# Wider first pieces of the MLP weights, and a fourth MLP unit ahead of the folds

One Trainium2 chip, one core of it. The metric is the device time of one execution in microseconds (us); an execution takes some 1.7 us more than the span of its instructions in the trace, and the tables say which is meant.

## The reference

A layer norm feeds two branches over the same 2048 tokens of width 640, and the sum of both with the residual is the output.

```
xn = layernorm(x)                                # x: 1 x 2048 x 640, bf16
# branch A: linear attention, 32 heads of 20
q, k, v = split(xn @ wqkv)
pq, pk  = q @ w_phi, k @ w_phi                   # per head, 20 x 20
phi(p)  = concat(softmax(p), softmax(-p))
o       = phi(pq) @ (phi(pk)^T v) / (phi(pq) @ sum(phi(pk)))
A       = o @ wo
# branch B: gated MLP, 1536 columns
B       = (silu(xn @ w1) * (xn @ w3)) @ w2
out     = x + A + B
```

The kernel folds w_phi into wq and wk (a "fold" multiplies a transposed 128-column chunk of wk with the block-diagonal w_phi), so that k and pk need one projection. A V tile is the ten matmuls that give v for 128 tokens, a K tile the ten that give pk for 128 tokens. A DMA transfer "lands" when all of its data has arrived.

## The kernel before

The program declares operations with a priority and lets its own list scheduler, with a model of durations and a random seed, put them into one order per engine at build time. On the chip that order is fixed. One MLP unit is ten matmuls: 128 columns of w1 and 128 of w3 against 512 tokens of xn transposed.

```
def mlp(b, fc, level):
    ...
    for j, w in enumerate((w1_s, w3_s)):
        for i in range(DC):                      # DC = 5 chunks of 128 rows
            mm(j, lambda k, j=j: bank(k + j), w[:, i, fc * 128:(fc + 1) * 128],
               xnT[:, i, b * 512:(b + 1) * 512], i == 0, i == DC - 1)
        ...                                      # tanh on ScalarE, products on VectorE
```

The head of the load order on the one SyncEngine queue, which is where the change sits:

```
    load_wv(4, 5, lv - 3)
    on_act(2.65, load_x, 3, 4)
    n = len(P.all)
    load_w13(0, 384, lv - 4)                     # first piece of w1, then of w3
    for d in P.all[n:]:
        d.raw.add(chunk)                         # not before the first piece of wv
    first = [P.all[n]]
    for e in range(DC):
        o = load_wT(1, e, lv - 9 - e, first)     # wk, transposed by the DMA; waits for w1's piece
        if e == 1:
            load(phi_s[:], phi_t, lv - 10.5, "SP", first)
    load_x(4, 8, lv - 19, "SP", [o])             # not before the last wk
    n = len(P.all)
    load_w13(384, 768, lv - 20)
    load_x(8, 12, lv - 21)
    ...
        if t in TURNED:                          # TURNED = (0,): tile 0 of xn
            turn(xnT[:, :, t * 128:(t + 1) * 128], x_tok[:, t, :], 2e6)   # by the DMA, same queue
        else:
            xn_transpose(t, ...)                 # tiles 1 to 3: on TensorE
```

The scheduler puts the transpose of tile 0 of xn behind the first w1 and w3 pieces in that queue. The first MLP unit needs all four tiles.

The softmax here doesn't subtract the row's maximum and nothing guards it: scores larger than these inputs give would overflow.

## Time and profile before

| kernel before | value |
|---|---|
| time, first three timed runs | 273.64, 273.80, 273.84 us |
| time of the run that was profiled first | 274.61 us (span 272.9) |
| TensorE (PE) busy | 98% of the span |
| first MLP matmul / first fold / first K tile | 13.17 / 19.65 / 22.25 us |

PE is the bound and is packed from the first K tile to the end, so the time is set by what happens ahead of that tile. The lines of the profile are in the prediction. (The MLP's first record is lost; 13.17 is worked out there.)

### The profile page before, as it was taken

The numbers are of one execution on the slowest core, as the hardware profiler recorded it, in microseconds if no ns is written. First come the engines' busy times: TensorE is split into PE (matmuls) and PEld (weight loads), VectorE is DVE, ScalarE is ACT, GpSimd is POOL, SyncE is SP. The second block draws the span as 40 slices with busy tenths as digits, with TensorE's granted clock in tenths as the row PEclk, the third lists the DMA queues.
The fourth block names the chain that finished last, engine by engine and source line by source line (L and its number), as shares of the span: only waits on it lengthen the run. The fifth ranks groups of instructions, "written<-read, shape, count | busy, mean of one in ns | idle before, by whom it ended". The sixth has DMA issues, their size and how long they took to land.

```text
span 272.9 us, 5057 instructions
## 1 busy us (share of the span) xinstructions
PE 266.8 (98%) x2076; PEld 158.9 (58%) x2095; DVE 181.4 (66%) x324; ACT 103.9 (38%) x194; POOL 61.0 (22%) x101
## 2 busy tenths in 40 slices
PE   8999999999999999999999999999999999999996
PEld 4747447777654446644544446677677774444774
DVE  5756999999998445469789978677661215666112
ACT  6637736777554541255493571010000002222000
POOL 4320643599999800000000000000000000000000
PEclk9999999999999999999999999999999999999999
DMA  7977999773000000712041131343332122000001
GB/s 221 191 98 241 342 221 157 116 168 112 0 0 2 0 0 4 228 62 32 19 50 24 26 49 24 82 113 78 96 98 79 67 73 73 0 0 0 26 24 48
DMA packets 41959, 22.14 MB, mean 81 GB/s; under 512 B 27728, under 2 KB 41936, under 8 KB 41936
## 3 DMA queue, kind: packets, MB, share of 16 engines
q1 hardware_dynamic: 41360, 21.17, 32.9%
q10 hardware_dynamic: 576, 0.66, 0.7%
q8 instruction: 16, 0.26, 0.4%
q14 instruction: 7, 0.06, 0.1%
HBM read 12.81 MB, written 2.62 MB: 57 GB/s over the span
## 4 chain that ended last, share of the span: by engine, by line
PE 82%; DMA 5%; POOL 4%; DVE 3%; SPq 2%; issue 2%; ACT 1%
PE PS L619 82%; POOL ekt L627 3%; SPq L693 2%; DMA w_s<-in_B_w_dram 2%; DMA wv<-in_A_wqkv_dram 1%; DMA wqkT<-in_A_wqkv_dram 1%; ACT EqT L627 1%; POOL mv L627 1%; DVE S L627 1%; DVE v L627 1%; DVE rS L627 1%; SPq L689 0%; DVE x_tok L627 0%; DVE Wqp L627 0%; DVE xres L627 0%
## 5 line engine op out<-in xcount | busy, mean ns | idle before, releaser
L619 PE MATMUL PS<-xnT,w_s 128*128 128x512 bf16 x465 | 105.1, 379 | 1.2 <-issue 0.5
L619 PEld LDWEIGHTS PS<-xnT,w_s 128*128 128x128 bf16 x480 | 46.3, 98 | 54.8 <-issue 0.3
L627 ACT ACTIVATE th<-PS 128x512 f32<-128x512 f32 x48 | 28.6, 597 | 71.2 <-PE PS L619 71.2
L619 PE MATMUL PS<-w_s,hT 128*128 128x320 bf16 (+2 forms) x384 | 55.0, 299 | 0.0
L627 DVE SCALAR_TENSOR_TENSOR t<-th,PS 128x512 bf16<-128x512 f32 x48 | 32.6, 682 | 26.2 <-ACT th L627 26.1
L619 PEld LDWEIGHTS PS<-w_s,hT 128*128 128x128 bf16 x384 | 37.1, 98 | 14.9
L627 DVE TENSOR_TENSOR xres<-PS,xres 128x640 bf16<-128x640 f32 (+2 forms) x17 | 13.4, 786 | 41.0 <-PE PS L619 41.0
L627 POOL TENSOR_TENSOR ekt<-ekt,rS 128x640 bf16<-128x640 bf16 x32 | 39.4, 1265 | 1.1 <-DVE rS L627 1.1
L627 DVE SCALAR_TENSOR_TENSOR hT<-t,PS 128x512 bf16<-128x512 bf16 x48 | 32.5, 680 | 1.1
L627 ACT ACTIVATE EqT<-PS 128x512 bf16<-128x512 f32 x40 | 22.0, 594 | 13.1 <-PE PS L619 13.0
L619 PE MATMUL PS<-wo_s,oT 128*128 128x320 bf16 (+2 forms) x160 | 24.5, 299 | 0.0
L627 DVE TENSOR_TENSOR prod<-PS,g_s 128x1280 bf16<-128x1280 f32 x16 | 23.9, 1491 | 0.5
L619 PE MATMUL PS<-Wkp,xnT 128*128 128x320 bf16 x160 | 23.9, 299 | 0.0
L627 ACT ACTIVATE ekt<-PS 128x640 bf16<-128x640 f32 x32 | 20.7, 699 | 7.4 <-PE PS L619 7.2
L619 PE MATMUL PS<-xnT,Wqp 128*128 128x512 bf16 x96 | 23.0, 379 | 0.4 <-issue 0.3
L627 DVE TENSOR_REDUCE S<-ekt 128x64 f32<-128x1280 bf16 x16 | 22.8, 1452 | 0.0
L627 ACT ACTIVATE e_s<-PS 128x64 f32<-128x64 f32 x32 | 9.1, 284 | 35.2 <-PE PS L619 34.8
L619 PEld LDWEIGHTS PS<-wo_s,oT 128*128 128x128 bf16 x160 | 15.7, 98 | 6.1
L619 PEld LDWEIGHTS PS<-Wkp,xnT 128*128 128x128 bf16 x160 | 15.5, 98 | 5.9 <-ACT Wkp L627 0.2
L619 PE MATMUL PS<-wv,xnT 128*128 128x320 bf16 x120 | 18.3, 299 | 0.0
L627 DVE BATCH_NORM_STATS2 bst<-x_tok 128x6 f32<-128x320 bf16 x32 | 14.3, 469 | 4.2 <-DMA x_tok<-in_A_x_dram 4.2
L619 PEld LDWEIGHTS PS<-xnT,Wqp 128*128 128x128 bf16 x100 | 9.3, 98 | 10.8
(67 smaller groups left out, 168.3 us busy)
## 6 DMA issues: line engine op xcount, KB each, us to landing
w_s<-in_B_w_dram SPq DMA_DIRECT2D x8, 480.0 KB, 6.8
xres<-in_A_x_dram SPq DMA_DIRECT2D x16, 160.0 KB, 2.2
out_dram<-xres SPq DMA_DIRECT2D x15, 160.0 KB, 1.8
x_tok<-in_A_x_dram SPq DMA_DIRECT2D x3, 640.0 KB, 7.6
w_s<-in_B_w_dram SPq DMA_DIRECT2D x1, 1920.0 KB, 9.2
wo_s<-in_A_wo_dram SPq DMA_DIRECT2D x1, 800.0 KB, 5.3
x_tok<-in_A_x_dram SPq DMA_DIRECT2D x2, 160.0 KB, 3.4
x_tok<-in_A_x_dram ACTq DMA_DIRECT2D x2, 160.0 KB, 3.7
```

The costliest lines, as they stand in the source:

```text
L619: return nc.tensor.matmul(o(u.k), l, r, start=start, stop=stop, skip_group_check=shared)
L627: return getattr(e, name)(*[at(a, u) for a in args], **{k: at(v, u) for k, v in kw.items()})
L693: d = P.dma("SP", lambda: nc.sync.dma_start_transpose(o, i), sb(o), sb(i), *pieces(o, 256), 1.31, level, after)
```

## The change

It wants the wait of the folds for the transposed wk to vanish: load 512 columns of w1 and w3 at first instead of 384, so that four MLP units rather than three can go ahead of the folds, and tell the scheduler that the wk transposes land 2.4 us after their data (1.0 before), so that it does place a fourth. A new seed picks another of the scheduler's random orders.

```
-SEED = 230
+SEED = 135
...
-    load_w13(0, 384, lv - 4)
+    load_w13(0, 512, lv - 4)
...
         o = load_wT(1, e, lv - 9 - e, first)
+        o.extra = 2.4
...
-    load_w13(384, 768, lv - 20)
+    load_w13(512, 1024, lv - 20)
     load_x(8, 12, lv - 21)
-    load_w13(768, 1152, lv - 22)
+    load_w13(1024, 1536, lv - 22)
     load_x(12, 16, lv - 23)
-    load_w13(1152, 1536, lv - 24)
```

## The prediction

> **What bounds the kernel now.** I read the page first: the engine table and the rows of 40 slices.
>
> ```profile
> PE 266.8 (98%) x2076; PEld 158.9 (58%) x2095; DVE 181.4 (66%) x324; ACT 103.9 (38%) x194; POOL 61.0 (22%) x101
> ...
> PE   8999999999999999999999999999999999999996
> ...
> PEclk9999999999999999999999999999999999999999
> DMA  7977999773000000712041131343332122000001
> ```
>
> TensorE (PE) is busy for 98% of 272.9 us at full clock, and only the first and the last slice are below nine tenths. The end of a matmul is modelled, though, so I also looked at the spacing of starts. After 22 us, start to start, I found the spacing of the shape everywhere except some 0.1 us at each switch between full-array and split-array matmuls, and a few holes of exactly one matmul, which are lost records (2095 weight loads, 2076 matmuls). So the kernel is a packed PE stream with a head. Moving work about inside the stream changes nothing; only idle time in the head can be won or added. The timeline of PE shows the head:
>
> ```profile
> 11.66 1.52 PE L619 MATMUL PS<-wv,xcT 128*128 128x320 bf16 x10
> 13.39 6.42 PE L619 MATMUL PS<-xnT,w_s 128*128 128x512 bf16 x29 [0.21 <-issue]
> 19.65 0.57 PE L619 MATMUL PS<-BDc,wqkT 128*128 128x140 bf16 x5
> 20.93 1.48 PE L619 MATMUL PS<-BDc,wqkT 128*128 128x140 bf16 x25 [0.71 <-DMA wqkT<-in_A_wqkv_dram]
> 22.25 5.60 PE L619 MATMUL PS<-Wkp,xnT 128*128 128x320 bf16 x40
> ```
>
> The last V tile of the first four is followed by three MLP units (29 of 30 matmuls recorded), the five folds of wk (5 + 25 matmuls), then four K tiles. The folds stop for the last transposed wk. Two rows further down price the pieces where nothing waits:
>
> ```profile
> 63.73 0.48 PE L619 MATMUL PS<-BDc,wqkT 128*128 128x140 bf16 x6
> 64.04 1.52 PE L619 MATMUL PS<-Wkp,xnT 128*128 128x320 bf16 x10
> ...
> 74.52 2.32 PE L619 MATMUL PS<-xnT,w_s 128*128 128x512 bf16 x10
> 76.68 1.52 PE L619 MATMUL PS<-wv,xnT 128*128 128x320 bf16 x10
> ```
>
> From start to start one fold takes 64.04 - 63.73 = 0.31 us and one MLP unit 76.68 - 74.52 = 2.16 us. Hence the folds before hold 22.25 - 19.65 - 5 x 0.31 = 1.05 us of waiting. The MLP began at 19.65 - 3 x 2.16 = 13.17 us, not at 13.39: its first record is lost.
>
> The chain of waits says what those waits hang on:
>
> ```profile
> 5.16 5.61 DMA w_s<-in_B_w_dram
> 10.77 0.02 issue
> 10.79 1.17 SPq L693
> ...
> 17.27 3.53 DMA wqkT<-in_A_wqkv_dram
> 20.80 0.14 issue
> 20.93 6.92 PE PS L619 x65
> ```
>
> The queue waits for the first w1 piece (10.77), then issues five transposes of wk and w_phi one by one until 18.5 us; the last lands at 20.80. Finally, the issues by themselves, one window each (w1 issued at 5.16, w3 at 5.58, the transpose of tile 0 of xn at 6.30), in us to landing:
>
> ```profile
> w_s<-in_B_w_dram SPq DMA_DIRECT2D x1, 480.0 KB, 5.6
> ...
> w_s<-in_B_w_dram SPq DMA_DIRECT2D x1, 480.0 KB, 6.7
> ...
> xnT<-x_tok SPq DMA_TRANSPOSE x1, 6.6
> ```
>
> They land at 10.8, 12.3 and 12.9 us. The V tile's last matmul starts at 12.88 and the first MLP matmul, which needs all of xn's four tiles, follows 0.24 us after the landing of tile 0. That transpose has no slack at all: this is the number the prediction turns on.
>
> **What the Trainium skill says.** "DMA: Bandwidth & Descriptors", section "Queues, rings and completion order": each DMA engine consumes one queue's descriptors in ring order. The trace agrees: the small transpose of xn lands 0.7 us behind w3 although it was issued 6 us earlier, so it inherits all growth of w1 and w3. The same page, "Why small descriptors are slow (HBM only)": a packet has a fixed cost beside its bytes. In the packet records the median is 36 ns for 768 bytes and 55 ns for 1,280, that is 19 ns per 512 bytes on a fixed part, which agrees. "TensorE: Matmul & The Clock Gate", section "Back-to-back issue gap": 512 columns take 512/2.4 + 2.5 = 216 ns when isolated; the 2.16 us for ten agree, and the page's sustained 131 ns is not seen here. Its section "HAM oscillation" warns of idle gaps above some 3.4 us; the gaps here are about 1 us and the clock row stays at nine, so I charge nothing for the clock.
>
> **The change, part by part.**
>
> 1. The first w1 and w3 pieces grow from 384 to 512 columns, 480 to 640 KB each. They remain 640 rows each, so 40 packets per engine; a packet grows from 768 to 1,024 bytes. Estimate by the line between the two measured sizes: 36 + 19/2 = 45.5 ns. One piece costs 40 x 9.5 ns = 0.38 us more, both 0.76 us. In the trace the last engine to finish w3 runs 768-byte packets back to back until 11.9 us, so I charge all of it. w1 lands at about 11.15, w3 at 13.0, tile 0 of xn at 12.93 + 0.76 = 13.7.
> 2. The first MLP matmul then starts at 13.17 + 0.76 = 13.93. This part costs **0.76 us**, on the path.
> 3. Four MLP units instead of three precede the folds (the order of instructions shows 40 matmuls where 30 were; the K tiles, six more units and the first mixed V and K tiles follow as before). They end at 13.93 + 4 x 2.16 = 22.57.
> 4. The transposes of wk start 0.38 us later with w1, up to 0.76 if the data behind them counts: last landing 21.2 to 21.6. The last fold inputs are needed at about 22.8. No wait: this part saves **1.05 us**. The extra 2.4 us given to them in the schedule is only a planning number and costs nothing itself.
> 5. The folds end at 22.57 + 1.55 = 24.12. The kernel before, with one more unit ahead, would be at 22.25 + 2.16 = 24.41. Difference **-0.29 us**.
> 6. Columns come in three pairs of 640 KB instead of four of 480: 3 x 40 packets per engine and matrix at 45.5 ns (5.5 us) instead of 4 x 40 at 36 (5.8 us), beside the stream. The second pair is wanted by the fifth unit, after folds and four K tiles: before, these K tiles took 27.68 - 22.25 = 5.43 us (one record lost at 27.9), so w1 at 24.12 + 5.43 = 29.6 and w3 half a unit later, 30.6. Before, the x load landed at 25.1 and the pair at 26.6 and 28.1, 1.5 us a piece. With x 0.6 us later and 1.5 x 45.5/36 = 1.9 us a piece they land at 27.6 and 29.5. It fits. Charge 0.
> 7. The tail is reordered by the new seed: one unit fewer before the sum over K and V, one more later. GpSimd's normalising ends at 91.5 us, PE's sum starts at 106.5; one unit of 2.16 earlier still leaves 12 us. The number of switches of array mode stays. Charge 0.
>
> Sum: 273.8 - 0.3 = **273.5 us**.
>
> **The rivals.**
> (a) The wait is fully won and the first MLP unit isn't delayed, because only the slowest DMA engine was behind and another run treats it better: then -1.05, 272.8. Against it: the transpose of xn had zero slack and queue order.
> (b) The wait merely moves and grows: w1, w3 and the transposes come later by more than 1.05 us, either through a slower packet or through the idle stretch of the DMA engines around 11 us, which I cannot explain from bytes. The break-even of the first MLP start is 24.41 - 1.55 - 8.64 = 14.22; a later one makes the time is 273.9 to 274.5. For it: landing times of transposes scatter by over 1 us (3.0 to 4.7 us from issue to landing).
> (c) The bigger second pair lands late and MLP unit five waits: up to +0.7, 274.2. Against it: the DMA engines have spare time then and w3 has 1 us more.
> (d) The new order opens holes in the second half, by VectorE's evictions (29.4 of the 30 us from 30 to 60 busy) or PSUM banks. Before, PE covers them all; PE's lead is the same afterwards. I give it +0.5 at worst.
>
> **Range and chances.** All terms are below 1.1 us, 0.4% of the time; three runs of before differ by 0.2. Eight in ten: 272.8 to 274.3, rivals (a) and (b) at its ends. Two per cent would be 5.5 us, five times the total idle time in the head, and a loss of that size needs a stall that no part of the change explains. Faster 0.005, same 0.985, slower 0.01.
>
> **What would show it.** In the timeline of PE: the gap ahead of the first MLP matmuls about 0.8 us longer, 40 of them, then 30 fold matmuls in one stretch with no wait on the transposed wk, K tiles from about 24.1. Landings: w1 near 11.2, w3 13.0, tile 0 of xn 13.7, last wk below 21.7. The sum over K and V about 2.4 us earlier than 106.5. It is wrong if the first MLP unit starts at 13.2 or after 14.3, if a fold still waits, or if PE waits on w_s near 30 us or on evictions later.

## The result, and the profile after

| | median | all runs, us |
|---|---|---|
| before, six runs | 273.77 | 273.62 to 274.39 |
| changed | 274.02 | 273.12, 273.96, 273.96, 274.09, 274.47, 278.03 (slow) |

The ratio is the mean time of the changed kernel's fast runs over that of the fast runs of before of the same rounds, so not quite the ratio of the medians: 1.0003, 95% interval 0.9983 to 1.0022. The time is the same. What is not the same is the spread: one run of six took 278 us, and the profile of the changed kernel is of that run. It lies 1.8% above the fastest, counts as slow and is left out of the ratio; further runs of 275.6 to 276.8 us, met below, count as fast and are in. It shows in one picture what can go wrong. Slow runs included, the mean of all 14 runs of the changed kernel in this document is 274.8 us against 274.0 for 34 of before (medians 274.2 and 273.9). First the page of the slow run, engine table and 40 slices:

```profile
PE 270.5 (98%) x2096; PEld 160.0 (58%) x2096; DVE 182.4 (66%) x325; ACT 103.2 (37%) x193; POOL 60.6 (22%) x101
...
PE   8969999999999999999999999999999999999996
...
PEclk9979999999999999999999999999999999999999
```

The third slice, 13.8 to 20.7 us, has a hole in PE and a lower clock; all others are as before. The timeline of PE gives it a name (columns: start, length, engine, line, operation, tiles, count, and in brackets the idle time and what ended it):

```profile
12.15 1.52 PE L619 MATMUL PS<-wv,xcT 128*128 128x320 bf16 x10
16.05 10.48 PE L619 MATMUL PS<-xnT,w_s 128*128 128x512 bf16 x40 [2.38 <-DMA xnT<-x_tok]
26.37 1.82 PE L619 MATMUL PS<-BDc,wqkT 128*128 128x140 bf16 x30
28.04 4.17 PE L619 MATMUL PS<-Wkp,xnT 128*128 128x320 bf16 x29
```

As intended, 40 MLP matmuls stand ahead of 30 fold matmuls that run in one stretch. The wait has moved ahead of the MLP, to the transpose of tile 0. And the four units took 26.37 - 16.05 = 10.3 us instead of 8.6. The windows show why (column PEclk, after POOL's, is the granted share of the clock):

```profile
16.00:17.00 1.00, 0.95 (x5) 0.43 (x6) 0.00 (x0) 0.00 (x0) 0.00 (x0) 0.92 0.75 97
17.00:20.00 3.00, 3.00 (x9) 1.04 (x8) 0.83 (x2) 0.60 (x1) 1.97 (x5) 0.50 0.58 119
20.00:21.00 1.00, 1.00 (x6) 0.44 (x5) 0.55 (x1) 0.00 (x0) 0.00 (x0) 0.88 0.64 141
```

After the idle gap the clock stood at half for 3.4 us. From the first K tile on, the changed kernel takes 276.3 - 28.04 = 248.3 us; before took 272.9 - 22.25 = 250.65 with one MLP unit (2.16) more in it, which makes 248.5. So the reordered stream behind the head costs nothing, and gains some 0.1 to 0.2 us. The whole question lies in the first 28 us.

### The profile page after: what moved, and what is told of

The parts are those of the page before. It is cut to its first block, busy times and chain, and to the rows that moved or that the text cites. A ratio compares the mean times of both kernels' runs of the same rounds, so it can differ in the third digit from the quotient of the medians.

```text
span 276.3 us, 5080 instructions
## 1 busy us (share of the span) xinstructions
PE 270.5 (98%) x2096; PEld 160.0 (58%) x2096; DVE 182.4 (66%) x325; ACT 103.2 (37%) x193; POOL 60.6 (22%) x101
## 3 DMA queue, kind: packets, MB, share of 16 engines
q1 hardware_dynamic: 40048, 21.17, 33.2%
## 4 chain that ended last, share of the span: by engine, by line
PE 93%; DMA 5%; SPq 0%; issue 0%; DVE 0%; ACT 0%; ACTq 0%
PE PS L619 93%; DMA xnT<-x_tok 3%; DMA x_tok<-in_A_x_dram 2%; SPq L689 0%; DVE xres L627 0%; ACT junk L627 0%; ACTq L1223 0%
## 5 line engine op out<-in xcount | busy, mean ns | idle before, releaser
L619 PE MATMUL PS<-xnT,w_s 128*128 128x512 bf16 x480 | 108.6, 384 | 2.4 <-DMA xnT<-x_tok 2.4
L627 ACT ACTIVATE ekt<-PS 128x640 bf16<-128x640 f32 x32 | 20.8, 701 | 8.6 <-PE PS L619 8.4
L619 PE MATMUL PS<-xnT,Wqp 128*128 128x512 bf16 x100 | 23.6, 380 | 0.0
```

What stands on the lines that cost most here:

```text
L619: return nc.tensor.matmul(o(u.k), l, r, start=start, stop=stop, skip_group_check=shared)
L627: return getattr(e, name)(*[at(a, u) for a in args], **{k: at(v, u) for k, v in kw.items()})
```

## The experiments

All were correct. Unless said otherwise an edit is made after the scheduler has run, on the finished order, so that nothing else in any engine's order moves. Before was timed with each: 11 runs beside the first four (median 273.89, 273.38 to 274.83) and 11 beside the rest (273.89, 273.62 to 275.31). A table of all runs stands at the end. The first four experiments ran on one chip, the others on a second; each group has its own runs of before.

**The changed kernel again**, no edit. 

> The changed kernel unchanged, for its spread and a profile in the fast state. Queue theory (the bigger w1 and w3 pieces hold back the transpose of tile 0 of xn in the same queue, and this eats the fold wait that is won): 273.1 to 274.6 us, mean near 273.9, spread wider than before's 0.7 us; first MLP matmul at 13.6 to 14.6 us, waiting for that transpose; no wait in the folds; from the first K tile to the end within 0.3 us of before less one MLP unit (250.65 - 2.16 = 248.5). Order theory (the head gains 0.3 us or more, and the reordered stream behind it gives it back): same time, but from the first K tile to the end 0.3 us or more above 248.5.

Measured: 273.23, 273.26, 273.53, 275.63, 276.40, 276.82 us; ratio of fast runs 1.0032 (0.9990 to 1.0075). The two groups are plain. The profiled run was 273.23:

```profile
11.61 1.52 PE L619 MATMUL PS<-wv,xcT 128*128 128x320 bf16 x10
13.19 8.58 PE L619 MATMUL PS<-xnT,w_s 128*128 128x512 bf16 x39
21.60 1.82 PE L619 MATMUL PS<-BDc,wqkT 128*128 128x140 bf16 x30
23.27 0.91 PE L619 MATMUL PS<-Wkp,xnT 128*128 128x320 bf16 x5
```

Here nothing waits: ten V matmuls, 40 MLP (one record lost, they begin at about 12.97), 30 fold matmuls, K at 23.27, and 271.5 - 23.27 = 248.2 to the end. My expectation that even this run would wait for tile 0 failed: with the wider pieces it landed at 12.7 us (issued at 6.17, 6.5 us to landing), in time. The issues of the queue in both runs, in order (start, length; the first wk is issued as soon as w1's piece has landed), the good run first, then the slow one:

```profile
5.17 0.95 SPq L689 DMA_DIRECT2D w_s<-in_B_w_dram  x2
6.17 1.44 SPq L693 DMA_TRANSPOSE xnT<-x_tok  x1
10.15 2.48 SPq L693 DMA_TRANSPOSE wqkT<-in_A_wqkv_dram  x2
```

```profile
4.79 0.95 SPq L689 DMA_DIRECT2D w_s<-in_B_w_dram  x2
6.47 2.27 SPq L693 DMA_TRANSPOSE xnT<-x_tok  x1
11.97 3.19 SPq L693 DMA_TRANSPOSE wqkT<-in_A_wqkv_dram  x2
```

The same bytes, and w1 lands at 10.1 in one run and at 12.0 in the other. So the time to land is not one number here; it scatters from run to run.

**The first w3 piece behind the transpose of tile 0**, in the changed kernel:

```
+    sp = [o for o in P.ops if o.nbytes and o.eng == "SP"]
+    w3, xt = sp[5], sp[6]
+    P.ops.remove(w3)
+    P.ops.insert(P.ops.index(xt) + 1, w3)
```

> The changed kernel with one edit: the first w3 piece is issued behind the transpose of tile 0 of xn, all else in the same order. Queue theory: the transpose lands at about 12 us, the first MLP matmul starts at 13.1 to 13.3 with no wait for it, w3 still lands by 14.2, no wait in the folds: 272.7 us, 1.0 under before, with a spread of 0.4 us or less. Order theory: 273.4 or more, since the stream behind the head is untouched. Accident theory (the landings scatter whatever the queue holds): 273.9 and the same spread as the changed kernel.

Measured: median 273.95, 273.49 to 274.83; ratio 1.0004 (0.9985 to 1.0023). No run of six is over 275, as the queue theory says. But the 1.0 us under before did not come: that expectation of mine fell, and with it the claim that before usually loses 1.05 us in its folds. The profile of this run (273.90):

```profile
12.27 1.52 PE L619 MATMUL PS<-wv,xcT 128*128 128x320 bf16 x10
13.84 8.58 PE L619 MATMUL PS<-xnT,w_s 128*128 128x512 bf16 x39
22.26 1.82 PE L619 MATMUL PS<-BDc,wqkT 128*128 128x140 bf16 x30
```

The MLP follows the V tile at once. It is the last V tile that starts 0.66 us later than in the run above (12.27 against 11.61). So a third thing, ahead of everything that the change touches, moves the time.

**Size alone**: the kernel before, its first pieces 512 columns and the second 256. 

> The kernel before with only its first w1 and w3 pieces 512 columns wide (the second 256): three MLP units ahead of the folds as before. Queue theory: first MLP matmul 0.76 us later, at about 13.9; folds start at 20.4 and still wait 0.3 to 0.7 us for the last wk; K tiles from 22.6 to 23.1; time 274.1 to 274.6. Accident theory: 273.8 as before.

```
+    ...                                               # the helper cut; sp: the queue's loads
+    for n, c0, c1 in ((4, 0, 512), (14, 512, 768)):   # n: place in the queue
+        cut(sp[n], w1_s, w1_t, c0, c1)                # load these columns instead
+        cut(sp[n + 1], w3_s, w3_t, c0, c1)
```

Measured: 273.38, 274.02, 274.04, 274.35, 275.51, 275.82; ratio 1.0021 (0.9995 to 1.0048). The profiled run (274.02) started its first MLP unit at 13.6 us, not 13.9, and because its V tile ended late, not for the transpose; its folds did not wait at all (K tile at 21.80). Two of six runs are above 275.5, where before had one in 34 over 275 (275.31). Six runs alone don't show that the size brings them; the table at the end counts all.

**Order of the queue alone**: the kernel before with w3 behind the transpose, the edit as above. 

> The kernel before with only the first w3 piece issued behind the transpose of tile 0 of xn. Queue theory: the first MLP matmul starts no more than 0.15 us earlier (it was just in time), the folds wait as long as before or 0.1 us longer: 273.6 to 273.8. If it gains 0.5 us or more, the transpose gates more of the kernel before than I read from its profile.

Measured: median 273.57, 273.31 to 274.20; ratio 0.9988 (0.9974 to 1.0003), a gain of 0.3 us that the interval doesn't separate from none. Its folds did not wait either: wk's last chunk landed at 18.5 us, and K began at 21.17. Within the expected "transpose was just in time", wrong on "the folds wait as long as before", and so on the time by a little.

These four made me drop the wait in the folds as a usual cost. The next four tested that, and the size.

**The kernel before again**, no edit. 

> The kernel before, unchanged, against itself: a second profile and the null spread. Theory now (the fold wait of 1.05 us that I read from the first profile is not typical: that profile took 274.6 us, the timed runs 273.8): no or under 0.5 us wait in the folds, first K tile at 21.1 to 21.8, 273.4 to 274.8 us, no run over 275. If the folds wait 0.8 us or more again, the wait is typical and the change must have lost its gain elsewhere in every run.

Measured: median 274.19, 273.67 to 274.84, ratio to itself 1.0007. The profiled run (274.18):

```profile
5.93 0.98 PE L619 MATMUL PS<-wv,xcT 128*128 128x320 bf16 x6 [0.62 <-DMA wv<-in_A_wqkv_dram]
...
12.41 1.52 PE L619 MATMUL PS<-wv,xcT 128*128 128x320 bf16 x10
13.77 6.64 PE L619 MATMUL PS<-xnT,w_s 128*128 128x512 bf16 x30
20.24 1.86 PE L619 MATMUL PS<-BDc,wqkT 128*128 128x140 bf16 x30
21.94 2.34 PE L619 MATMUL PS<-Wkp,xnT 128*128 128x320 bf16 x16
```

The 30 fold matmuls took 21.94 - 20.24 = 1.70 us where the first profile had 2.60: no wait. wk landed at 19.5 us, before it was wanted. Most of what this run lost, it lost at 5.9 us to a late piece of wv; its K tile is 0.14 us past the range that I expected, and one of the 11 runs of before beside it took 275.31 where I expected none over 275. The fold wait that the change removes was there in the one profile I had predicted from, and in none of the three later profiles of before or of before with one edit.

**The dose doubled**: the changed kernel with first pieces of 640 columns, the second 384. 

> The changed kernel with its first w1 and w3 pieces 640 columns wide (the second 384), all else in place: the dose doubled. Queue theory (the pieces hold back the transpose of tile 0): the first MLP matmul at 13.5 us or later and waiting for that transpose; half or more of the runs over 275 us, median 275 or more. Accident theory (slow runs have nothing to do with the size): 2 or fewer of 6 over 275, median 274.0 to 274.6 as the changed kernel.

```
+    ...                                               # cut and sp as above
+    for n, c0, c1 in ((4, 0, 640), (14, 640, 1024)):
+        cut(sp[n], w1_s, w1_t, c0, c1)
+        cut(sp[n + 1], w3_s, w3_t, c0, c1)
```

Measured: 273.89, 274.22, 274.87, 277.96, 278.57, 279.25; median 276.41, the three long ones with a mean clock of 0.993 or 0.994 (the long runs of the changed kernel, 275.6 to 276.8, kept 1.0; its 278.03 had 0.994). Two of the three count as slow and are left out of the ratio, 1.0044 (0.9995 to 1.0092), which therefore says little here. The profiled run, 274.87, waited for tile 0 and started its MLP at 14.3 us. Half of the runs over 275, as the queue theory asked. The accident theory allowed two of six, so this arm alone speaks against it by one run (and by the median).

**The same four units, 384 columns ahead of the transpose**, and the other 128 columns of w1 and w3 as two loads right behind it:

```
+    ...
+    w1.emit, w3.emit = cut(w1_s, w1_t, 0, 384), cut(w3_s, w3_t, 0, 384)
+    spot = P.ops.index(xt) + 1                  # xt: the transpose of tile 0
+    for j, w, src in ((0, w1_s, w1_t), (1, w3_s, w3_t)):
+        o = _Op({"SP": (cut(w, src, 384, 512), 0.45, 0.0)})
+        o.emit, o.nbytes = cut(w, src, 384, 512), 1
+        P.ops.insert(spot + j, o)
+        fourth.mms[5 * j].raw.add(o)            # fourth: the MLP unit that reads them
```

> The changed kernel with its order and its four units, but only 384 columns of w1 and w3 ahead of the transpose of tile 0, and the other 128 columns of each in two loads right behind it. Queue theory: no run over 275 us, median 273.2 to 273.7; first MLP matmul as in before (12.9 to 13.2), no wait in the folds. If runs over 275 us stay, it is the order or the later loads that make them, not the size ahead of the transpose.

Measured: median 273.90, 273.35 to 274.06; ratio 0.9990 (0.9972 to 1.0009). No run over 275; the median is a little above what I expected. The seed, the order and the four units of the change are kept, and no slow run came. At the changed kernel's rate (5 of 14, all its runs), six runs without one would still come up by chance in 7 cases of 100, so this arm needs the others beside it; together they are counted below.

**Both**: 384 columns of w1, the transpose, 384 of w3, then the remainders.

```
+    P.ops.remove(w3)                            # and the edit of the split, behind w3
+    P.ops.insert(P.ops.index(xt) + 1, w3)
```

> As the split, and the first w3 piece behind the transpose too: w1 (384), transpose, w3 (384), then the two loads of 128 columns. Meant to beat both: the transpose lands by 11.5 us, w3 by 13.5, the fourth columns by 18, no wait on PE from the V tiles to the K tiles. 273.1 to 273.6 us, spread under 1 us; 0.1 us or more under the split if tile 0 still gates there.

Measured: median 273.93, above the 273.1 to 273.6 that I expected, 273.21 to 274.24; ratio 0.9994 (0.9973 to 1.0015). The landings came as expected (transpose 10.2, w3 12.4, last columns 13.7 us). PE waited for nothing between the V and the K tiles, and still this does not beat before: in three of the four profiles of before's order (two of them with an edit) the folds don't wait either.

**Four more**, one run each, to catch slow runs with a profile. The changed kernel: 

> The changed kernel once more, one look, in the hope of a profile of a run over 275 us (4 of 12 were). Queue theory: if it is over 275, its first MLP matmul starts 1.5 us or more after the last V matmul, waiting for the transpose of tile 0, and the stream from the first K tile to the end is unchanged (270.4 - 2.16 = 248.2 within 0.3 us); if it is at 273.2 to 274.5, that gap is under 0.6 us. Rival: the slow runs lose their time somewhere behind the K tiles.

> The changed kernel again, a second look, same expectations as the first look: gap ahead of the first MLP matmul, start of the V stage and half clock account for the excess over 273.2 us within 0.4 us.

The 640-column dose: 

> The 640-column dose once more, one look (3 of 6 were over 277.9). Queue theory: over 275 us it has a gap of 1.5 us or more ahead of the first MLP matmul behind a late transpose of tile 0, and where the granted clock is under 1, a stretch of half clock right after the gap; otherwise the gap is under 1 us. Rival: slow runs lose their time behind the K tiles.

> The same kernel again, a second look, same expectations: the gap ahead of the first MLP matmul, plus the matmuls at half clock after it, account for the whole excess over 273.3 us within 0.6 us.

Measured: 274.24 and 276.18 for the changed kernel, 274.58 and 278.60 for the dose. The run of 276.18:

```profile
11.69 1.52 PE L619 MATMUL PS<-wv,xcT 128*128 128x320 bf16 x10
15.91 8.79 PE L619 MATMUL PS<-xnT,w_s 128*128 128x512 bf16 x40 [2.70 <-DMA xnT<-x_tok]
24.55 1.82 PE L619 MATMUL PS<-BDc,wqkT 128*128 128x140 bf16 x30
26.21 4.04 PE L619 MATMUL PS<-Wkp,xnT 128*128 128x320 bf16 x28
```

A gap of 2.70 us with the clock kept: 2.94 us later at the K tile than the good run (26.21 against 23.27), and 276.18 - 273.23 = 2.95 us longer. The run of 278.60 had a gap of 2.91 and the half clock:

```profile
16.64 10.48 PE L619 MATMUL PS<-xnT,w_s 128*128 128x512 bf16 x40 [2.91 <-DMA xnT<-x_tok]
26.96 1.82 PE L619 MATMUL PS<-BDc,wqkT 128*128 128x140 bf16 x30
```

The run of 274.58 had a gap of 0.35 us. The run of 274.24 had none ahead of the MLP; it lost 0.61 us to a late wv:

```profile
7.46 1.01 PE L619 MATMUL PS<-wv,xcT 128*128 128x320 bf16 x4 [0.61 <-DMA wv<-in_A_wqkv_dram]
```

Of the four expectations one failed, on its sum: for 278.60 the gap (2.91) and the half clock (10.32 - 8.64 = 1.68) make 4.59 of the 5.3 us over 273.3, 0.7 short where I allowed 0.6. The last V tile of that run started at 12.21, 0.60 us later than in the good run. From the first K tile on nothing was lost in any of the four (248.2 to 248.3 us).

All runs together, counted over 275 us:

| kernel | columns of w1 + w3 ahead of tile 0 | over 275 us |
|---|---|---|
| before (all its runs) | 384 + 384 | 1 of 34 |
| before, w3 behind | 384 + 0 | 0 of 6 |
| before, 512 first | 512 + 512 | 2 of 6 |
| changed | 512 + 512 | 5 of 14 |
| changed, w3 behind | 512 + 0 | 0 of 6 |
| changed, split | 384 + 384 | 0 of 6 |
| changed, split, w3 behind | 384 + 0 | 0 of 6 |
| dose | 640 + 640 | 4 of 8 |

With 512 or more columns of both pieces ahead of tile 0, 11 of 28 runs are over 275 us, with less ahead 1 of 58; without the twelve runs that gave me the theory (the result and the first experiment) it is 7 of 16 against the same 1 of 58. The split shows in both groups of experiments, each on its own chip. No single row of six would settle it; for the last two counts together chance would do it in less than one case of 10,000. With packets just as wide but w3 behind the transpose there was none in six, so nothing points to the size of the packets by itself.

And the first K tile sets the time in every profile, read from the starts above and the spans (the eight profiles not in the table: 250.5 in the two of before's order, 248.2 to 248.5 in the six of the new order):

| profiled run | time | first K tile | from there to the end |
|---|---|---|---|
| before, first | 274.61 | 22.25 | 250.6 |
| before, again | 274.18 | 21.94 | 250.5 |
| changed, good | 273.23 | 23.27 | 248.2 |
| changed, with late wv | 274.24 | 24.27 | 248.2 |
| changed, gap | 276.18 | 26.21 | 248.3 |
| changed, gap and half clock | 278.03 | 28.04 | 248.3 |

## Why the prediction was right, and where it was not

The median lies in the range: 274.02 against 273.5, same. Two of the six runs do not lie in it (274.47 and 278.03), and the gain of 0.3 us did not come. The total is near the number by luck: the two terms that decide the sum were both wrong. Going through its steps:

- **What bounds the kernel.** Right. PE is packed behind the head in all profiles, and from the first K tile to the end the time is constant to some 0.1 us in each order (the dose's 274.87 is 0.3 us over).
- **Step 7, the tail, charged 0.** Nearly right: 250.6 - 2.16 - 248.25 = 0.2 us are won by the other order, 0.1 with the 250.5 of the other profiles.
- **Steps 3 and 6.** Right. 40 MLP matmuls stand ahead of the folds; the second pair of columns landed at 26.1 and 27.9 us in the good run and 27.7 and 29.6 in the first slow one (27.6 and 29.5 forecast), before it was wanted.
- **Steps 1 and 2, 0.76 us of cost on the path.** The place was right: the transpose of tile 0, behind the wider pieces in the queue, is what the first MLP unit waits for in all three long runs that were profiled (of twelve; the others are only counted). So was the price of a piece: the median packet of 1,024 bytes took 46 ns (45.5 estimated), and w3 landed 1.85 to 1.92 us behind w1 in all four profiles of the changed kernel, against 1.5 to 1.7 with 384 columns and 2.3 with 640. (A small misreading: w3's last 768-byte packet ended at 11.7 us, not 11.9.) What failed is to add 0.76 us to a fixed start. From issue to landing w1 took 5.0 to 7.2 us in these four profiles, and the V tile ends at its own time. In two of them tile 0 cost nothing (it landed before the V tile ended), in the two slow ones the gap was 2.4 and 2.7 us. The prediction called itself wrong if the first MLP unit started at 13.2 us or after 14.3; it started at 12.97, 13.97, 15.91 and 16.05, so by its own sign this step failed in three of four, and 13.97 was set by a late V tile.
- **Step 4, 1.05 us saved.** This term failed. The folds' wait is real in the first profile and removed, but it is not in the kernel's usual run: two profiles of before's order with one edit and a second one of before show none. I took it from a run of 274.61 us while the timed ones stood at 273.8, and did not ask which 0.8 us of the profile were that run's own. It was mis-sized as well: five folds without a wait take 1.70 us in those three profiles, not 5 x 0.31 = 1.55, so the first profile held 0.9 us of waiting. Its chain shows what made it wait: w1 landed at 10.77, 5.6 us after its issue, and the wk transposes are issued behind it; in the other three w1 took 4.1 to 4.5 us and the last wk landed at 18.5 to 19.5 instead of 20.8. So both terms hang on the same scatter of w1. The sum -0.29 came out near the truth because both were overrated together, which is luck.
- **The clock, charged nothing.** Wrong in two of the three long runs that were profiled. There the four units took 1.7 us longer (10.32 against 8.64).
- **Rival (a)**, fully won and nothing delayed, describes the good runs' trace, but not their time: there was nothing to win. Rival (b), the wait moves and grows, describes the long ones, and beyond its upper end of 274.5. Rivals (c) and (d) did not show in any run.

Left open is why the landing jumps. In the two long profiles of the changed kernel fifteen of w1's sixteen parts had landed by 10.4 us and the last came at 11.8 and 12.0; in the dose's long profile three came late, at 11.4 to 12.2. In the other profiles with both wide pieces ahead of the transpose w1 was complete at 10.1 to 11.2. Then a 16 KB packet of the instruction queue, 1.03 to 1.06 us long, starts at 13.6 to 14.3 us while the transpose is unfinished, and of the transpose's 16 parts one lands and the other fifteen follow 1.1 to 1.2 us later; in the other profiles all parts land within 0.15 to 0.4 us. That would fit a collision of the two, but why one packet should hold up fifteen parts I can't say, and it was not tested: no run moved the instruction fetch. Nor do I know why the last part of w1 falls behind; in these three runs w1 was issued early (4.8 to 4.9 us), but so it was in one run of the dose without a large gap.

Open too is the spread of 0.7 us or more that all kernels share. Two parts of it are in the profiles: a late piece of wv (0.62 and 0.61 us of wait at 5.9 and 7.5 us), and the time at which the clock opens, seen in how long the five transposing matmuls at 4.6 us take:

```profile
4.33 0.45 PE L814 MATMUL PS<-ident,xc 128*128 128x128 bf16 x5
```

```profile
4.64 0.74 PE L814 MATMUL PS<-ident,xc 128*128 128x128 bf16 x5
```

The first is the good run of the changed kernel, the second the run with w3 behind, where the V tile came 0.66 us later.

## What to carry to other kernels

Before pricing a wait from one profile, compare that run's time with the timed ones: a wait of 1 us in a run that is 0.8 us slow may belong to the run and not to the kernel. A small transfer that gates the first work waits here for every byte ahead of it in its queue, and their cost is not the mean alone: what the extra bytes bought was a long run in three (7 of 20 with 512 columns). Where PE is otherwise packed, one late landing can cost twice, for the gap and, as in two of three profiles here, for the half clock after it.

## What the Trainium skill lacked or had wrong

- "TensorE: Matmul & The Clock Gate", "HAM oscillation": it warns of idle gaps over some 3.4 us. Here gaps of 2.38 and 2.91 us were followed by 3.4 us at half clock, one of 2.70 us was not. So a gap under the figure is no safety. All complete clock records here last a whole number of times 3.41 us (3.41, 10.24, 256.0 in the result's run), which fits the page's free-running window of that length. In both halved runs one such stretch, 13.4 to 16.8 us, holds the whole gap and the half clock follows it; for the third run no clock record was kept, so whether its gap fell across two stretches stays open.
- The same page, Part 1: the opening of the clock is given as about 4 us into sustained matmul work with 0.5 us either way, though the same Part calls the number of slow matmuls run-variable. By the clock records it opened here at 3.6 us in one run and at 6.8 us in another, with the first filler matmul at 0.84 in both: 2.7 and 6.0 us.
- "DMA: Bandwidth & Descriptors": no section, and no other page of the skill, gives the time that an instruction fetch takes on the DMA engines. The packet records here show 16 KB packets of 0.9 to 1.6 us, sixteen in a run.
- The same page fits a transfer's time as a fixed cost plus bytes over a rate (for the other issuing path), with no spread. The first w1 piece of 640 KB, at the same place in the program, took from 5.0 to 7.2 us to land in four profiles of the changed kernel.
